# One layernorm a slot sooner, mixer pieces cut 2-3-0, the last rest products moved, and a copy moved to VectorE, in a fused attention, mixer and MLP kernel

## The chip, the cores and the metric

One NeuronCore of a Trainium2 chip runs the whole kernel. The metric is the device time of one launch in microseconds. Engines are called as in the profile: PE (TensorE matmul; PEld its weight loads), DVE (VectorE), ACT (ScalarE), POOL (GpSimd) and SP (SyncE, which here only issues DMAs).

## The reference

With 2048 rows of 576 columns in bf16:

```python
xn = layernorm(A_x)
# A: attention of 32 query heads over 16 cached key/value heads, the last 512 keys of 2048
q  = (xn @ wq).reshape(B, Sq, 32, 128)
p  = softmax(einsum(q, k) * 128 ** -0.5)
s  = (p @ v).reshape(B, Sq, 4096) @ wo
# B: mixer, then MLP
h  = gelu(layernorm(xn) @ w1)
hs = concat(the four quarters of h's columns, shifted by 1, -1, 2, -2 rows) @ w2
x1 = xn + hs
h2 = gelu(layernorm(x1) @ w3) @ w4          # 576 -> 4608 -> 576
out = A_x + s * silu(x1 + h2)
```

## The kernel before

The rows are worked in four blocks of 512. The first part of the program is attention with the mixer woven in, the second the MLP with the final product. A block and a query head make a unit; there are U = 128 of them (4 blocks x 32 heads), and the loop at L787 gives each a slot `u`, numbered from 0, with two more stretches behind the last.

In slot u PE does, in this order: the first of four scores matmuls of unit u (`stage_s`, L471: keys of 128 positions times q, each followed by an exp on ScalarE), the q projection of unit u+1 (`stage_q`, L448), the second scores, half of the value products of unit u-1 (`stage_v`, L484; 16 matmuls in all, each of which reads the exps), the third scores, the other half, and the fourth scores. What is called scores 0 to 3 in the prediction are these four. Scores have three PSUM banks, q and the mixer's pieces share two (`ps_pq`). 576 is four times 128 and 64 more: the last 64 rows of q's weights, the rest rows, are done for four heads at once (`rest_q`, L435), in every fourth slot from slot 7 on; it takes a q bank and two scores banks more, and in these slots the second scores stand right behind the first (`trip`, L693). Slot 127 has no q projection.

Other work is laid into the slots by hand. `fill` holds what is done after the first scores (layernorm steps, transposes, loads); `pe_fill` holds lists of PE matmuls, which the loop cuts into thirds and puts behind the second, third and fourth scores. Such lists are the output projection (`wo_atoms`, 32 matmuls a list, the last list 128), the mixer's first products `b1` (five matmuls to a piece, whose last starts the gelu chain `gelu1`: a cast and four more steps on VectorE around a tanh on ScalarE), and its second products `b2` (five matmuls to a tile) with `b2_rem` (20 matmuls, the last 64 columns, then one add and the store of x1). The mixer works on xnnT, the transposed result of the second layernorm: `ln2_steps` writes xnn_b on VectorE from slot `ln2_at[b]` on, three steps to a slot, and `tr2` (L555) has SP issue one DMA transpose for 128 rows, in the slots `tr2_at[b]`. Block 1's first piece stands in slot Hq + 12 = 44 (Hq is 32). At the end of each slot SP is given the DMA transpose of a finished head's output (`stage_t`, oT), which the output projection of the block reads from 32 slots later on.

SP, POOL and PE run in the order written (L786). The order on VectorE and ScalarE is a planner's, by its own costs and by priorities; exps have none, q's copies, the value results and the gelu chain have a raised one. At the start, up to L785, all engines run in the order written. There `ln1_first` (L358) normalizes the first block, and PE transposes it (`tr1_first`, L401), between transposes of the keys (`keys_first`). The tile xn has 640 columns: 576 and a second copy of the last 64 (`D:DP`), the rest columns; the copy was computed on POOL for each of the four groups of 128 rows.

Of the kernel before, what the change touches and what calls it, by code (L numbers as in the profile page):

```python
# [8 lines left out]
P = 128  # L9
ACT = mybir.ActivationFunctionType  # L10
ALU = mybir.AluOpType
# [20 lines left out]
def kernel(  # L32
# [14 lines left out]
    nc = tc.nc  # L47
# [3 lines left out]
    _, S, D = A_x.shape  # L51
    _, Hkv, Sk, Dh = A_k_cache.shape
    assert Dh == P
    Hq = A_wq.shape[1] // Dh
# [8 lines left out]
    NB = S // QB  # L63
    TB = QB // P
    SCALE = float(Dh) ** -0.5
    NF = D // P
    DR = D - NF * P
    NDC = NF + 1
    DP = NDC * P
# [26 lines left out]
    def rows(ap, t0, n):  # L96
        return ap[t0 * P:(t0 + n) * P, :].rearrange("(tt p) d -> p tt d", p=P)
# [110 lines left out]
    with ExitStack() as actx:  # L208
# [97 lines left out]
        def late(ap, fn):  # L306
            g = nc.gpsimd.tensor_copy(out=gate[:, :], in_=ap)
            with tc.issue_after(g.ins):
                fn()
# [48 lines left out]
        def ln1_first():  # L358


            x, xn = x_t.pop(0), xn_b[0]
            xn_t[0] = xn
            root = float(D) ** 0.5
            mv = small.tile([P, TB, 2], FP32, name="ln_mv")
            nb = small.tile([P, 1], FP32, name="nr_e")
            y = small.tile([P, TB], FP32, name="nr_y")
            scrap = wo_sb[:, 0:2, :].rearrange("p a b -> p (a b)").bitcast(FP32)
            t = TB - 1
            nc.scalar.activation(out=y[:, 0:1], in_=eps_t[:], func=ACT.Sqrt)
            nc.scalar.activation(out=scrap, in_=x[t], func=ACT.Copy, scale=-1.0 / (D * root), accum_out=nb[:])  # L370
            nc.scalar.activation(out=scrap, in_=x[t], func=ACT.Square, scale=1.0 / root, bias=nb[:],
                                 accum_out=mv[:, t, 1:2])
            hw = D // 2
            for i in range(t):
                st = small.tile([P, 2, 6], FP32, name="ln_st")
                for j in range(2):
                    nc.vector.bn_stats(out=st[:, j, :], in_=x[i][:, j * hw:(j + 1) * hw])
                nc.vector.bn_aggr(out=mv[:, i, :], in_=st[:])
                if i == 1:
                    nc.scalar.activation(out=y[:, 0:2], in_=mv[:, 0:2, 1], func=ACT.Sqrt, bias=eps_t[:])  # L380
            nc.vector.tensor_scalar(out=mv[:, t, 0:1], in0=nb[:], scalar1=-root, scalar2=None, op0=ALU.mult)
            nc.scalar.activation(out=y[:, 2:4], in_=mv[:, 2:4, 1], func=ACT.Sqrt, bias=eps_t[:])
            e = small.tile([P, 1], FP32, name="nr_e")
            nc.scalar.activation(out=e[:], in_=nb[:], func=ACT.Exp, scale=0.0)
            for i in range(TB):
                if i % 2 == 0:
                    nc.vector.reciprocal(out=y[:, i:i + 2], in_=y[:, i:i + 2])
                nc.gpsimd.tensor_scalar(out=xn[:, i, D:DP], in0=x[i][:, NF * P:D], scalar1=mv[:, i, 0:1],
                                        scalar2=y[:, i:i + 1], op0=ALU.subtract, op1=ALU.mult)
                nc.vector.tensor_scalar(out=xn[:, i, 0:D], in0=x[i], scalar1=mv[:, i, 0:1], scalar2=y[:, i:i + 1],  # L390
                                        op0=ALU.subtract, op1=ALU.mult)
            return mv

        def transpose_tile(dstT, src, tt):
# [156 lines left out]
        def ln2_steps(b):  # L551
            return layernorm_steps(small, [xnn_b[:, tt, 0:D] for tt in range(TB)],
                                   [xn_t[b][:, tt, 0:D] for tt in range(TB)])

        def tr2(b, tt):  # L555
            transpose_tile(xnnT, xnn_b, tt)
# [45 lines left out]
        def b2_shift(b):  # L602
            with tc.high_priority(offset=HP):
                b2_shift_(b)
# [10 lines left out]
        def b2_mm(ps, b, tt, c, lo, hi):  # L615
            if c < 4:
                o0 = PAD - SHIFT[c] + tt * P
                lhsT = hb_t[b][:, c, o0:o0 + P]
            else:
                lhsT = hs_t[b][:, tt * P:(tt + 1) * P]  # L620
            nc.tensor.matmul(ps, lhsT=lhsT, rhs=w2_sb[:, c, lo:hi], start=(c == 0), stop=(c == 4))  # L621
# [15 lines left out]
        def b2_rem(b):  # L637
            st = {}

            def mm(tt, c):  # L640
                if tt == 0 and c == 0:
                    st["ps"] = ps_pq.tile([P, TB, R0], FP32, name="psx1r", tag="pq")
                b2_mm(st["ps"][:, tt, :], b, tt, c, M0, D)
                if tt == TB - 1 and c == 4:
                    with tc.high_priority(offset=HP):
                        nc.vector.tensor_tensor(out=x1o_t[b][:, :, M0:D], in0=st["ps"][:, :, :],
                                                in1=xn_t[b][:, :, M0:D], op=ALU.add)
                    nc.sync.dma_start(out=rows(x1_dram, b * TB, TB), in_=x1o_t.pop(b)[:])
                    xn_t.pop(b)

            return [lambda tt=tt, c=c: mm(tt, c) for tt in range(TB) for c in range(5)]
# [19 lines left out]
        U = NB * Hq  # L671
        fill, pe_fill = {}, {}

        def at(u, fn):
            fill.setdefault(u, []).append(fn)

        def pe(u, atoms):
            pe_fill.setdefault(u, []).extend(atoms)
# [5 lines left out]
        def later(u, make, per):  # L684
            cell = []
            for i in range(2 * TB + 1):
                def step(i=i):
                    if not cell:
                        cell.append(make())
                    cell[0][i]()  # L690
                at(u + i // per, step)

        def trip(u):  # L693
            return PLAIN - 1 <= u < U - 1 and u % 4 == 3

        ln2_at = (7, Hq + 4, 2 * Hq - 4, 2 * Hq + 21)
        tr2_at = ((33, 33, 34, 34), (Hq + 8, Hq + 8, Hq + 9, Hq + 9),
                  (2 * Hq - 1, 2 * Hq - 1, 2 * Hq, 2 * Hq), (2 * Hq + 25, 2 * Hq + 25, 2 * Hq + 26, 2 * Hq + 26))
        b1_early = {Hq + 4: [(0, 0)], Hq + 5: [(0, 2)], Hq + 6: [(0, 4)]}
        b1_after = {Hq + 4: [(0, 1)], Hq + 5: [(0, 3)]}  # L700
# [4 lines left out]
        for c, u in enumerate((12, 13, 14, 16, 17)):  # L705
            b1_after[Hq + u] = [(1, c)]
        b2_at = ((Hq + 20, Hq + 21, Hq + 22, Hq + 24), (2 * Hq + 8, 2 * Hq + 9, 2 * Hq + 10, 2 * Hq + 12),
                 (3 * Hq + 8, 3 * Hq + 9, 3 * Hq + 10, 3 * Hq + 12), (4 * Hq - 4, 4 * Hq - 3, 4 * Hq - 2, 4 * Hq - 1))
# [12 lines left out]
        for b in range(NB):  # L721
            later(ln2_at[b], lambda b=b: ln2_steps(b), 3)
            for tt in range(TB):
                at(tr2_at[b][tt], lambda b=b, tt=tt: tr2(b, tt))
            at(b2_at[b][0] - 1, lambda b=b: b2_shift(b))
            for tt in range(TB):
                pe(b2_at[b][tt], b2(b, tt))
            pe(b2_at[b][TB - 1], b2_rem(b))
            if b + 1 < NB:
                at(x_at[b], lambda b=b: late(pT_t[x_at[b]][0][0:1, 0:1], lambda: load_x(b + 1, nc.gpsimd)))  # L730
                u1 = ln1_at[b]
                later(u1, lambda b=b: ln1_steps(b + 1), 3)
                for tt in range(TB):
                    at(u1 + (3 + tt // 2 if b else 5 + tt), lambda b=b, tt=tt: tr1(b + 1, tt))
# [24 lines left out]
        with tc.manual_schedule(engines={SP, POOL, PE, DVE, ACTE}):  # L759
            mv = ln1_first()  # L760
# [25 lines left out]
        with tc.manual_schedule(engines={SP, POOL, PE}):  # L786
            for u in range(0, max(max(fill), max(pe_fill)) + 1):  # L787
                atoms = pe_fill.get(u, []) + [fn for v, g in pe_late if v == u for fn in prep_k(g)]
                n = len(atoms)
                cut = [atoms[0:n // 3], atoms[n // 3:2 * n // 3], atoms[2 * n // 3:]]  # L790
                if u == 1:
                    stage_q(2)
                for i in range(4):
                    if u < U and not (i == 1 and trip(u)):
                        stage_s(u, i)
                    if i == 0:
                        if trip(u):
                            stage_s(u, 1)
                        if 1 < u < U - 1:
                            stage_q(u + 1)  # L800
                        for fn in fill.get(u, []):
                            fn()
                        continue
                    if i < 3 and 0 <= u - 1 < U:
                        stage_v(u - 1, 2 * (i - 1))
                    for fn in cut[i - 1]:
                        fn()
                if 0 <= u - 1 < U:
                    stage_t(u - 1)


    with ExitStack() as bctx:
# [184 lines left out]
        with tc.manual_schedule(engines={PE, DVE, ACTE}):  # L997
# [7 lines left out]
            for d in range(0, ND, 2):  # L1005
                b = d // NP
# [56 lines left out]
            b = NB - 1  # L1063
# [49 lines left out]
    with tc.If(flag > 0):  # L1113
        with ExitStack() as gctx:
# [19 lines left out]
            with tc.For_i(0, NT, 1) as t:  # L1134
# [3 lines left out]
                xn = work.tile([P, D], BF16, name="r_xn")  # L1138
# [6 lines left out]
                for h in range(Hq):  # L1145
                    g = h // REP
                    if h % REP == 0:
                        k_nat = work.tile([P, KCH, Dh], BF16, name="r_k")
                        nc.sync.dma_start(out=k_nat[:],
                                          in_=A_k_cache[0, g, K0:, :].rearrange("(kc p) d -> p kc d", p=P))  # L1150
                        v_g = work.tile([P, KCH, Dh], BF16, name="r_v")
                        nc.sync.dma_start(out=v_g[:],
                                          in_=A_v_cache[0, g, K0:, :].rearrange("(kc p) d -> p kc d", p=P))
# [80 lines left out]
```

## Time and profile before

| | before |
|---|---|
| time, median of 3 runs | 834.55 us (833.75 to 834.86) |
| the profiled execution | 833.96 us, its span 832.2 us |
| instructions | 19602 |
| granted TensorE clock | 0.998 |
| DMA | 83.95 MB, mean 101 GB/s |

The span runs from the first to the last instruction. Attention with the mixer takes the first 510 us, the last block's output projection follows up to 541, and the MLP runs from there to 825 us. In the timelines the columns are: start in us, duration in us, engine, line, operation, out<-in, shape, count; in brackets the idle time of the engine ahead of it and what ended it. SPq and POOLq stand for issues by these engines' queues. The end of a matmul is modelled, and matmuls overlap; their starts are recorded.

### The profile page before, as it was taken

How to read it: one execution, taken by the hardware profiler on the slowest of the kernel's cores; microseconds unless marked ns; L12 is line 12 of the kernel's file. 1: busy time of each engine (PE TensorE's matmuls, PEld its weight loads, DVE VectorE, ACT ScalarE, POOL GpSimd, SP SyncE). 2: the span in 40 equal slices, each digit the busy share in tenths (PEclk: the TensorE clock that was granted, in tenths of full speed). 3: DMA queues.
4: the chain of work that ended last, by engine and by line, in shares of the span. 5: the costliest groups of instructions: out<-in, count | busy, mean ns of one | idle time of the engine just before them, and what ended most of it. 6: DMA issues, size and time to landing. Idle time of an engine off the chain costs nothing.

```text
span 832.2 us, 19602 instructions
## 1 busy us (share of the span) xinstructions
PE 821.2 (99%) x7974; PEld 470.8 (57%) x7974; DVE 471.7 (57%) x1430; ACT 457.1 (55%) x819; POOL 98.7 (12%) x166
## 2 busy tenths in 40 slices
PE   9999999999999999999999999999999999999996
PEld 6666655655554565655465655555555555555555
DVE  5778635768884367964346774043246636546333
ACT  6888853578783368984467983042233333335600
POOL 5343313010100111110001100000000000000000
PEclk9999999999999999999999999999999999999999
DMA  7988992363472135772044364992000411230101
GB/s 202 188 180 187 188 170 74 85 116 71 98 148 57 41 91 124 136 139 49 12 84 128 99 112 96 313 329 34 2 28 18 98 36 45 48 87 23 37 18 44
DMA packets 141024, 83.95 MB, mean 101 GB/s; under 512 B 107504, under 2 KB 133808, under 8 KB 140928
## 3 DMA queue, kind: packets, MB, share of 16 engines
q1 hardware_dynamic: 130128, 53.01, 31.7%
q0 software_dynamic: 9408, 28.15, 12.3%
q8 instruction: 64, 1.05, 0.6%
q10 hardware_dynamic: 1392, 1.48, 0.5%
q14 instruction: 32, 0.26, 0.1%
HBM read 49.17 MB, written 9.44 MB: 70 GB/s over the span
## 4 chain that ended last, share of the span: by engine, by line
PE 97%; DVE 1%; POOL 1%; ACT 1%; issue 1%; DVEq 0%; POOLq 0%; ACTq 0%
PE ph L884 14%; PE po L494 14%; PE pswo L518 13%; PE psq L456 13%; PE sc L477 13%; PE pm L921 11%; PE pm L1086 4%; PE ph L570 3%; PE pm L884 2%; PE psx L621 2%; PE pswr L518 2%; PE pr L921 1%; PE psq L441 1%; PE sc L441 1%; PE pr L1086 0%
## 5 line engine op out<-in xcount | busy, mean ns | idle before, releaser
L479 ACT ACTIVATE pT<-sc 128x512 bf16<-128x512 f32 x512 | 287.4, 598 | 105.5 <-PE sc L477 97.4
L477 PE MATMUL sc<-qT,kT 128*128 128x512 bf16 x512 | 175.6, 379 | 0.0
L494 PEld LDWEIGHTS <-pT 128*128 128x128 bf16 x2048 | 134.5, 98 | 54.7 <-issue 9.8
L494 PE MATMUL po<-v_sb,pT 128*128 128x129 bf16 x2048 | 158.2, 220 | 0.3 <-ACT pT L479 0.3
L456 PE MATMUL psq<-xT_b,wq_b 128*128 128x512 bf16 x520 | 132.9, 379 | 0.0
L884 PE MATMUL ph<-xT_b,w_s 64*128 64x512 bf16 x976 | 127.1, 376 | 0.4 <-DVE hx L900 0.4
L921 PE MATMUL pm<-w_s,h 64*128 64x512 bf16 x864 | 122.3, 377 | 0.0
L518 PE MATMUL pswo<-wo_sb,oT 128*128 128x512 bf16 x512 | 116.6, 379 | 0.0
L499 DVE TENSOR_TENSOR o<-po,ri_b 128x256 bf16<-128x256 f32 x256 | 107.9, 422 | 6.2
L902 ACT ACTIVATE h<-ph 128x512 bf16<-128x512 f32 x67 | 39.4, 597 | 130.4 <-PE ph L884 130.4
L921 PEld LDWEIGHTS <-h 64*128 64x128 bf16 x1728 | 70.8, 94 | 55.6 <-issue 0.4
L518 PEld LDWEIGHTS <-oT 128*128 128x128 bf16 x1024 | 65.2, 98 | 56.9 <-DMA oT<-o 0.3
L921 PE MATMUL pr<-w_s,h 64*128 64x64 bf16 x864 | 90.2, 189 | 0.2 <-ACT h L902 0.2
L884 PEld LDWEIGHTS <-w_s 64*128 64x128 bf16 x1152 | 57.3, 94 | 48.9 <-issue 0.8
L456 PEld LDWEIGHTS <-wq_b 128*128 128x128 bf16 x520 | 50.5, 98 | 59.5 <-issue 1.0
L900 DVE COPY hx<-ph 128x512 f32<-128x512 f32 x55 | 38.0, 691 | 70.0 <-PE ph L884 70.0
L498 DVE RECIPROCAL ri_b<-po 128x2 f32<-128x2 f32 x256 | 42.2, 165 | 52.9 <-PE po L494 48.9
L477 PEld LDWEIGHTS <-kT 128*128 128x128 bf16 x512 | 47.0, 98 | 24.5 <-DVE qT L464 0.6
L265 POOL DMA_DIRECT2D wq_b<-in_A_wq_dram x30 | 23.3, 777 | 293.4 <-PE sc L477 273.9
L464 DVE TENSOR_TENSOR qT<-psq,rq 128x512 bf16<-128x512 f32 x60 | 41.4, 690 | 23.6 <-ACT pT L479 13.2
L466 DVE CAST qT<-psq 128x512 bf16<-128x512 f32 x44 | 30.3, 688 | 34.4 <-PE psq L441 27.3
L874 DVE TENSOR_SCALAR fence<-ph,ph 1x1 f32<-1x1 f32 x61 | 12.8, 209 | 51.7 <-PE ph L884 51.1
(151 smaller groups left out, 755.3 us busy)
## 6 DMA issues: line engine op xcount, KB each, us to landing
wq_b<-in_A_wq_dram POOLq DMA_DIRECT2D x30, 512.0 KB, 4.8
wo_sb<-in_A_wo_dram POOLq DMA_DIRECT2D x8, 576.0 KB, 5.3
w_s<-in_B_w_dram SPq DMA_DIRECT2D x9, 512.0 KB, 7.1
w_s<-in_B_w_dram SPq DMA_DIRECT2D x10, 288.0 KB, 5.1
x_dram<-x SPq DMA_DIRECT2D x4, 576.0 KB, 3.4
x<-x_dram SPq DMA_DIRECT2D x4, 576.0 KB, 4.2
w_s<-in_B_w_dram SPq DMA_DIRECT2D x4, 576.0 KB, 7.7
s_b<-s_dram SPq DMA_DIRECT2D x4, 576.0 KB, 5.0
```

Source lines behind the costliest of these rows:

```text
L456: nc.tensor.matmul(psq[:, :], lhsT=w[:, kc, hh * Dh:(hh + 1) * Dh], rhs=xT_b[qb % 2][:, kc, :], start=(kc == 0 and not (two and hh == 1)), ...
L464: nc.vector.tensor_tensor(out=qT[:, :], in0=psq[:, :], in1=rq_t.pop(u)[:, :], op=ALU.add)
L477: nc.tensor.matmul(sc[:, :], lhsT=kT[:, g, kc * P:(kc + 1) * P], rhs=qT_t[u][:, :], start=True, stop=True)
L479: nc.scalar.activation(out=pT[:, :], in_=sc[:, :], func=ACT.Exp, scale=SCALE)
L494: nc.tensor.matmul(po[:, j, :], lhsT=pTs[kc][:, tt * P:(tt + 1) * P], rhs=v_sb[:, g, kc, 0:Dh + 1], start=(kc == 0), stop=(kc == KCH - 1))
L498: nc.vector.reciprocal(out=ri, in_=po[:, :, Dh])
L499: nc.vector.tensor_tensor(out=o[:, t0:t0 + 2, :], in0=po[:, :, 0:Dh], in1=ri.unsqueeze(2).to_broadcast([P, 2, Dh]), op=ALU.mult)
L518: nc.tensor.matmul(ps, lhsT=oT_t[qb * Hq + h][:, tt, :], rhs=wo_sb[:, h, lo:hi], start=(h == 0), stop=(h == Hq - 1))
L884: nc.tensor.matmul(ps[i][:, :], lhsT=lhsT, rhs=xT[half, kc, :], start=first, stop=last, skip_group_check=True)
L900: nc.vector.tensor_copy(out=src[:, :], in_=ps[i][:, :])
L902: nc.scalar.activation(out=h3[:, :], in_=src[:, :], func=ACT.Gelu_apprx_tanh)
L921: nc.tensor.matmul(out, lhsT=h3_t[b, fc][half, tt * P:(tt + 1) * P], rhs=w4_s[fc // WS][half, fc % WS, lo:hi], start=key not in started, s ...
```

## The change

- `ln2_at[1]` is 35 instead of 36 (the second layernorm of block 1), and `tr2_at[1]`, its four DMA transposes, 39, 39, 40, 40 instead of 40, 40, 41, 41.
- A list of exactly five matmuls is cut 2, 3, 0 instead of 1, 2, 2. This meets the mixer's pieces and tiles that stand alone in a slot.
- `b2_rem` of the last block leaves the thirds of slot 127 and stands in `fill` of slot 128, where it comes ahead of the value products of unit 127. Slot 127 then has a list of five.
- For row groups 2 and 3 of the first block POOL no longer computes the rest columns; VectorE copies them for both groups at once from columns 512 to 575 of the finished xn.

```diff
                 if i % 2 == 0:
                     nc.vector.reciprocal(out=y[:, i:i + 2], in_=y[:, i:i + 2])
-                nc.gpsimd.tensor_scalar(out=xn[:, i, D:DP], in0=x[i][:, NF * P:D], scalar1=mv[:, i, 0:1],
-                                        scalar2=y[:, i:i + 1], op0=ALU.subtract, op1=ALU.mult)
+                if i < 2:
+                    nc.gpsimd.tensor_scalar(out=xn[:, i, D:DP], in0=x[i][:, NF * P:D], scalar1=mv[:, i, 0:1],
+                                            scalar2=y[:, i:i + 1], op0=ALU.subtract, op1=ALU.mult)
                 nc.vector.tensor_scalar(out=xn[:, i, 0:D], in0=x[i], scalar1=mv[:, i, 0:1], scalar2=y[:, i:i + 1],
                                         op0=ALU.subtract, op1=ALU.mult)
+            nc.vector.tensor_copy(out=xn[:, 2:TB, D:DP], in_=xn[:, 2:TB, NF * P:D])
...
-        ln2_at = (7, Hq + 4, 2 * Hq - 4, 2 * Hq + 21)
-        tr2_at = ((33, 33, 34, 34), (Hq + 8, Hq + 8, Hq + 9, Hq + 9),
+        ln2_at = (7, Hq + 3, 2 * Hq - 4, 2 * Hq + 21)
+        tr2_at = ((33, 33, 34, 34), (Hq + 7, Hq + 7, Hq + 8, Hq + 8),
...
-            pe(b2_at[b][TB - 1], b2_rem(b))
+            if b + 1 < NB:
+                pe(b2_at[b][TB - 1], b2_rem(b))
+            else:
+                for atom in b2_rem(b):
+                    at(U, atom)
...
-                cut = [atoms[0:n // 3], atoms[n // 3:2 * n // 3], atoms[2 * n // 3:]]
+                c1, c2 = (2, n) if n == 5 else (n // 3, 2 * n // 3)
+                cut = [atoms[0:c1], atoms[c1:c2], atoms[c2:]]
```

## The prediction

> **What bounds the kernel now.** I read the page first, then the waits of PE, then the timeline at each place that the change touches.
>
> ```profile
> span 832.2 us, 19602 instructions
> PE 821.2 (99%) x7974; PEld 470.8 (57%) x7974; DVE 471.7 (57%) x1430; ACT 457.1 (55%) x819; POOL 98.7 (12%) x166
> ...
> L494 PE MATMUL po<-v_sb,pT 128*128 128x129 bf16 x2048 | 158.2, 220 | 0.3 <-ACT pT L479 0.3
> ```
>
> PE is never idle for long: 99% of the span. Nothing taken off DVE, ACT or POOL shortens the run by itself; only a place where PE stands still does. The change removes no matmul and adds none, so its whole worth is the sum of the PE pauses that it closes, less those that it opens. PE's waits name one large one in the attention phase:
>
> ```profile
> PE ph L570 <- issue: 1.4, 1, 1.4
> ```
>
> It is the first matmul of block 1's first mixer piece (slot 44). The timeline around it (start, duration, engine, line):
>
> ```profile
> 148.59 1.45 DVE L136 TENSOR_SCALAR xnn_b<-xn_b,ln_mv,nr_y 128x576 bf16<-128x576 bf16 x4
> ...
> 161.08 3.11 SPq L507 DMA_TRANSPOSE oT<-o  x2
> 164.24 2.59 SPq L395 DMA_TRANSPOSE xnnT<-xnn_b  x2
> 166.94 1.20 SPq L507 DMA_TRANSPOSE oT<-o  x1
> 168.18 2.60 SPq L395 DMA_TRANSPOSE xnnT<-xnn_b  x2
> ...
> 169.12 0.79 POOL L265 DMA_DIRECT2D wq_b<-in_A_wq_dram  x1 [13.98 <-PE sc L477]
> ...
> 170.67 1.02 PE L456 MATMUL psq<-xT_b,wq_b 128*128 128x512 bf16 x4
> ...
> 172.16 0.63 PE L494 MATMUL po<-v_sb,pT 128*128 128x129 bf16 x8
> ...
> 174.81 0.62 PE L494 MATMUL po<-v_sb,pT 128*128 128x129 bf16 x8
> ...
> 176.81 0.38 PE L570 MATMUL ph<-xnnT,w_sb 128*128 128x512 bf16 x1 [1.38 <-issue]
> ```
>
> The matmul reads xnnT, written by four DMA transposes. Two answers on that tile say how long these took to land, first the third transpose, then the third and fourth together:
>
> ```profile
> L395 SPq DMA_TRANSPOSE xnnT<-xnn_b x1: 1275/1275/1275, 168.2 to 168.2; - x1
> DMA to landing us min/median/max: 2.6/2.6/2.6
> ...
> L395 SPq DMA_TRANSPOSE xnnT<-xnn_b x2: 1275/1276/1276, 168.2 to 169.5; - x2
> DMA to landing us min/median/max: 2.6/4.9/7.2
> ```
>
> The fourth, issued at 169.5, needs 7.2 us and lands at 176.7; PE goes on at 176.81. The third, one issue earlier, needed 2.6. Between them the load of wq begins (169.12). The layernorm is not late: its results were written by 150.0, 14 us before the first transpose. What is late is the transposes' place in SP's queue.
>
> **Part 1: second layernorm and transposes of block 1.** The eight value products from 174.81 show 0.62 us, one alone 0.22 (the page's row of L494): starts 0.057 apart, the last at 175.21, so PE could have gone on at 175.27. Lost: 176.81 - 175.27 = 1.54 us. SP's order after the projection's store is now oT, oT, two xnnT, oT, two xnnT; afterwards oT, two xnnT, oT, two xnnT, oT. The fourth xnnT moves ahead of one oT, whose issue holds SP for 1.2 to 1.3 us, so it is issued at about 168.2. That is the time at which the third went out before, and it then landed in 2.6: 170.8, or 4.5 us before PE asks. The wq load does not move, since it waits for PE (its row). I take the full 1.54. The oT transposes that are passed go out later and meet the load in its place; block 1's output projection reads them only from slot 65 on. The layernorm's VectorE work is the same and has 14 us of slack. If the cover fails (issue after 169.1), the whole 1.54 stays. The edit frees nothing else: next late are the two pauses of part 2.
>
> A page speaks to the size. The Trainium skill (Trainium Kernel Development and Optimization, Performance Expectations) calls matmul busy time a bad metric because matmuls are pipelined. By the idle time of the row, 1.38, the sum below would be 0.16 smaller; the starts, which the trace has for every matmul, decide for 1.54.
>
> **Part 2: five-matmul pieces in two thirds of a slot.** A slot runs: scores 0, q, scores 1, half of the value products, third one, scores 2, other half, third two, scores 3, third three. Five matmuls were cut 1, 2, 2 and become 2, 3, 0. This concerns 18 slots (44 to 46, 48, 49, 52 to 54, 72 to 74, 104 to 106, 124 to 127). From 170.67 the four q matmuls show 1.02 us, the last one 0.38, so starts are 0.215 apart. The piece's last matmul comes one step, 0.215, sooner; scores 3 comes two steps, 0.43, later; the slot is as long as before.
>
> For it: two pauses where every fourth slot takes the rest rows of q. An undisturbed one runs from its q matmuls to its value products in 172.16 - 170.67 = 1.49 us. Those of slots 47 and 51:
>
> ```profile
> 186.62 1.03 PE L456 MATMUL psq<-xT_b,wq_b 128*128 128x512 bf16 x4
> 187.26 0.69 DVE L585 CAST g_x<-ph 128x512 bf16<-128x512 f32 x1
> 188.52 0.63 PE L494 MATMUL po<-v_sb,pT 128*128 128x129 bf16 x8
> ...
> 200.41 1.02 PE L456 MATMUL psq<-xT_b,wq_b 128*128 128x512 bf16 x4
> 200.51 0.63 ACT L591 ACTIVATE g_th<-g_u 128x512 bf16<-128x512 bf16 x1 [0.36 <-DVE g_u L589]
> 201.04 1.55 ACT L479 ACTIVATE pT<-sc 128x512 bf16<-128x512 f32 x3
> 202.47 0.63 PE L494 MATMUL po<-v_sb,pT 128*128 128x129 bf16 x8
> ```
>
> Slot 47 takes 1.90 (0.41 lost): q's second bank is the piece's, free when the cast ends at 187.95. Slot 51 takes 2.06 (0.57 lost): the tanh at 200.51 holds up three exps, and their banks are wanted. Both hang on the gelu chain, which starts with the piece's last matmul. Bounds: nothing (the chain is held by VectorE's order, or scores 3 comes too late in slot 46) to 0.98. A chain that is 0.215 sooner all through gives back 0.22 at each place, 0.43; the steps that a planner orders may give more or less. I take 0.45.
>
> Against it: the 0.43 by which scores 3 is late. Its exp starts 0.42 after the matmul and serves PE 0.65 after that (507.88, 508.30, 508.95 in the rows below): 1.07 in all. In an ordinary slot the value products that need it follow seven steps and three small ones later, 7 x 0.215 + 3 x 0.057 = 1.7: covered by ScalarE being at most 0.6 behind. In slot 46 it is busy 2.69 of 3.71 us:
>
> ```profile
> 182.48:186.19 3.71, 3.71 (x30) 2.18 (x29) 3.50 (x11) 2.69 (x5) 1.98 (x3) 1.00 0.32 75
> ```
>
> (after the window: its length, then PE, PEld, DVE, ACT). So I cost it at nothing there. Slot 127 has no q, and the cover is gone.
>
> **Parts 2 and 3 at the end of attention.** The rows of slots 127 and 128:
>
> ```profile
> 504.64 1.73 ACT L479 ACTIVATE pT<-sc 128x512 bf16<-128x512 f32 x3 [0.44 <-PE sc L477]
> 504.87 0.59 PE L477 MATMUL sc<-qT,kT 128*128 128x512 bf16 x2
> 505.31 0.62 PE L494 MATMUL po<-v_sb,pT 128*128 128x129 bf16 x8
> ...
> 507.88 0.38 PE L477 MATMUL sc<-qT,kT 128*128 128x512 bf16 x1
> 508.22 0.28 PE L621 MATMUL psx1r<-w_sb,hb 128*128 128x64 bf16 x4
> 508.30 0.60 ACT L479 ACTIVATE pT<-sc 128x512 bf16<-128x512 f32 x1 [0.24 <-PE sc L477]
> 508.36 0.33 PE L494 MATMUL po<-v_sb,pT 128*128 128x129 bf16 x3
> 508.95 0.91 PE L494 MATMUL po<-v_sb,pT 128*128 128x129 bf16 x13 [0.26 <-ACT pT L479]
> 509.02 0.36 SPq L648 DMA_DIRECT2D x_dram<-x  x1
> 509.50 3.00 SPq L507 DMA_TRANSPOSE oT<-o  x2
> ```
>
> Now: the third small value product starts at 508.47, the fourth could at 508.53 and waits until 508.95: 0.42 lost. The 20 rest products (64 columns, 0.03 apart by 508.22: 0.58 in all) stood 3, 8 and 9 in the thirds of slot 127; afterwards all stand behind scores 3. Behind it come one step, 0.58 and three small products, 0.97, against 1.07: 0.10 lost. So part 3 gains 0.32. But scores 3 of slot 126 is late by 0.43: its exp starts at 505.07 instead of 504.64, serves PE at 505.72, and the fourth value product from 505.31 wants it at 505.48. That opens 0.24. Net of the two at this place: 0.08. I take 0.1.
>
> On SP the store of x1 (509.02) falls from before the last two oT transposes to between them; it waits for one VectorE add behind the rest products. Behind it on SP stands only the last oT.
>
> **Part 4: rest columns on VectorE.** The start (PE's transposes of x, then q):
>
> ```profile
> 9.28 1.09 DVE L412 COPY xT_b<-ps_x 128x512 bf16<-128x512 bf16 x3 [0.90 <-PE ps_x L404]
> 9.36 0.10 PEld L404 LDWEIGHTS <-xn_b 128*128 128x128 bf16 x1 [0.18 <-POOL xn_b L388]
> 9.39 1.08 ACT L410 ACTIVATE xT_b<-ps_x 128x512 bf16<-128x512 bf16 x2 [0.93 <-PE ps_x L404]
> 9.88 2.32 PE L456 MATMUL psq<-xT_b,wq_b 128*128 128x512 bf16 x10
> ```
>
> One transpose waits 0.18 for POOL; that wait goes. But q's fourth matmul needs ScalarE's second copy, done at 10.47, and starts at 9.88 + 3 x 0.215 = 10.53. It cannot come 0.18 sooner, only about 0.03. VectorE's added copy (between nothing and the 0.42 of one of its copies here) lies in the 0.90 us in which VectorE waits. POOL's next work, a load of v, starts sooner by the two instructions that leave it; its heads come up many slots later. Bounds 0 to 0.18; I take 0.03, by the copy's row.
>
> **Sum.** 1.54 + 0.45 + 0.1 + 0.03 = 2.1 us. The profiled execution took 833.96 us (span 832.2, the rest outside it), the median of the three runs is 834.55. So a span of about 830.1, 831.9 for such an execution, and 832.4 on the median.
>
> **Rivals.**
> - *The pieces give nothing* (pauses at 47 and 51 stay, 0.1 at the end stays or goes): 1.5 to 1.7 us, 832.9. For it: the chain has planner-ordered steps between cast and tanh. Against: its first link is plainly PE. A part of it: the last oT was issued as the second of the 3.00 us at 509.50, and PE wants it 31 steps after 509.7, at 516.4; if it lands no sooner while PE comes sooner, the gain of part 3 returns as a wait.
> - *The transpose still meets the load*: issue slips past 169.1, it lands at 176.7, 1.54 is lost and 0.6 remains: 833.9. Against: SP's issues are back to back and one of them is taken from in front. The Trainium skill (DMA: Bandwidth & Descriptors, Queues, rings and completion order) says that each DMA engine takes turns between queues packet by packet, so any transpose unfinished when the load starts would be stretched; the 7.2 beside 2.6 agrees, and by that rule only an issue ahead of the load helps.
> - *Slower: late scores 3 everywhere.* If ScalarE is over 0.6 us behind at scores 3, each of the other 17 slots opens the 0.24 of slot 127: 4.1 us, net 2.0 slower, 836.5. For it: tanh and q copies share ScalarE in five of them. Against: 2.69 of 3.71 busy, and plain slots run scores 3 right before the next slot without a pause.
>
> **How the numbers follow.** Forecast 0.57, pieces give nothing 0.28, load still met 0.09, slower 0.06. The bound of 0.2% is 1.7 us, about what a measurement of this kernel can tell from no change. The forecast lies beyond it except for a twentieth (0.54), the first rival on either side of it (0.13 faster, 0.15 same), the second within. Faster 0.67, same 0.27, slower 0.06. Range: the pieces' full 0.98 and some scatter below, 831.4; the met load above, 833.9.
>
> **What would show it.** Right: no wait of ph L570 on issue; the fourth xnnT of block 1 issued near 168.2 and landed in under 3 us; slots 47 and 51 nearer 1.49 from q to value products; a new pause of about 0.24 in slot 127's first value products; q at the start moved by under 0.1. Wrong: a landing over 5 us for that transpose, or new pauses of PE before value products in slots 45 to 50, which would be the slower case.

## The result, and the profile after

| | before | after |
|---|---|---|
| median | 833.70 us (9 runs, 832.97 to 834.86) | 831.54 us (9 runs, 831.07 to 831.96) |
| profiled execution | 833.96 us, span 832.2 | 831.61 us, span 829.8 |
| ratio of the times | | 0.9972, 95% interval 0.9962 to 0.9983 |

By the medians the change saves 2.16 us; the ratio puts it at 0.28%. (The first three runs of before had 834.55, the median that the prediction was set against.) The top of the page after, and PE's waits after:

```profile
span 829.8 us, 19512 instructions
...
PE 816.6 (98%) x7888; PEld 471.4 (57%) x7974; DVE 472.8 (57%) x1431; ACT 455.3 (55%) x819; POOL 97.2 (12%) x164
```

```profile
PE ph L891 <- DVE hx L907: 0.4, 2, 0.2
PE pr L928 <- ACT h L909: 0.2, 1, 0.2
```

PE's busy time says nothing here: this trace lacks 86 matmul records (7888 against 7974). The weight loads (PEld) are complete, and all shifts below are taken from their starts, before against after. The wait of ph on issue is gone from the list, and with it the wait of po on pT at the end of attention; the shorter waits that came in its place are told below. Two waits of ph on hx are left, at 575 and 709 us; they play a part below.

**Block 1's transposes.** The third and fourth after:

```profile
L397 SPq DMA_TRANSPOSE xnnT<-xnn_b x2: 1275/1280/1285, 167.0 to 168.3; - x2
...
DMA to landing us min/median/max: 2.6/2.6/2.7
```

The fourth is issued at 168.3 and lands after 2.7 us where it took 7.2. From slot 44 to slot 45 the weight loads shift by 1.54.

**Slots 46, 47 and 51** (timeline after):

```profile
184.04 0.63 ACT L593 ACTIVATE g_th<-g_u 128x512 bf16<-128x512 bf16 x1 [0.82 <-DVE g_u L591]
...
184.57 2.04 ACT L481 ACTIVATE pT<-sc 128x512 bf16<-128x512 f32 x4
184.63 0.95 PE L479 MATMUL sc<-qT,kT 128*128 128x512 bf16 x3
...
185.42 1.02 PE L458 MATMUL psq<-xT_b,wq_b 128*128 128x512 bf16 x4
185.76 0.69 DVE L587 CAST g_x<-ph 128x512 bf16<-128x512 f32 x1
...
187.03 0.63 PE L496 MATMUL po<-v_sb,pT 128*128 128x129 bf16 x8
...
198.70 0.74 PEld L458 LDWEIGHTS <-wq_b 128*128 128x128 bf16 x4
198.74 0.63 ACT L593 ACTIVATE g_th<-g_u 128x512 bf16<-128x512 bf16 x1
...
200.70 0.63 PE L496 MATMUL po<-v_sb,pT 128*128 128x129 bf16 x8
```

Slot 47 now needs 187.03 - 185.42 = 1.61 us from q to its value products (1.90 before, 1.49 undisturbed). But on ScalarE the tanh of 184.04 now stands ahead of the exps of the third and fourth scores of slot 46: ScalarE waits 0.82 for the tanh's input, and four exps follow in a row from 184.57 on. (Before, the exp of the third scores ran at 184.92, ahead of the tanh at 185.66.) So the second scores of slot 47 find no free bank in time: they start at 185.21, when the exp of the third scores is done (185.15), 0.37 behind the first instead of the 0.22 of before, and q comes 0.15 late with them. Net gain at this place: 0.15. In slot 51 q's first weight load stands at 198.70, which puts its first matmul at 198.91 (0.21 later, as in slot 47: 185.21 and 185.42), so 1.79 us against 2.06: 0.27 gained.

**The end of attention** (timeline after):

```profile
503.34 1.57 ACT L481 ACTIVATE pT<-sc 128x512 bf16<-128x512 f32 x3 [0.66 <-PE sc L479]
...
503.57 0.88 PE L496 MATMUL po<-v_sb,pT 128*128 128x129 bf16 x8
503.99 0.28 PEld L496 LDWEIGHTS <-pT 128*128 128x128 bf16 x5 [0.26 <-ACT pT L481]
...
506.45 0.60 ACT L481 ACTIVATE pT<-sc 128x512 bf16<-128x512 f32 x1 [0.66 <-PE sc L479]
```

Eight value products take 0.88 instead of 0.62: the new pause of slot 127, 0.25, with its releaser named. In slot 128 the fourth value product, which needs the last exp, still waits 0.10 and starts at 507.10. Together the place gains 0.11 to 0.13.

**The start.** First before, then after:

```profile
9.25 1.75 POOL L288 DMA_DIRECT2D v_sb<-in_A_v_cache_dram  x2
```

```profile
8.11 1.75 POOL L288 DMA_DIRECT2D v_sb<-in_A_v_cache_dram  x2
...
8.51 0.57 DVE L393 COPY xn_b<-xn_b 128x128 bf16<-128x128 bf16 x1
...
8.79 0.86 PE L406 MATMUL ps_x<-ident,xn_b 128*128 128x128 bf16 x10
```

The moved copy takes 0.57 us, and PE's transposes wait for it for 0.12. The first q matmul starts at 10.00 instead of 9.88, but 0.10 of this is the first loads: PE's first transpose of x stands at 7.26 instead of 7.16. Counted from that transpose, the first q matmul comes 0.01 to 0.02 later, and q's third weight load and all behind it 0.13 later (3.07 against 2.94).

All shifts together, up to the last matmul (825.16 before, 823.33 after): 1.54 + 0.42 + 0.11 - 0.13, less the 0.10 by which the first loads landed later, is 1.84; the last matmul shows 1.83. The rest of the 2.35 us between the spans lies behind the start of the last matmul (7.03 us before, 6.50 after), where the profiles of all kernels here lie anywhere between 6.0 and 7.0.

### The profile page after: what moved, and what is told of

Its sections match the earlier page's. It is cut to its first block, busy times and chain, and to the rows that moved or that the text cites. A ratio compares the mean times of both kernels' runs of the same rounds, so it can differ in the third digit from the quotient of the medians.

```text
span 829.8 us, 19512 instructions
## 1 busy us (share of the span) xinstructions
PE 816.6 (98%) x7888; PEld 471.4 (57%) x7974; DVE 472.8 (57%) x1431; ACT 455.3 (55%) x819; POOL 97.2 (12%) x164
## 4 chain that ended last, share of the span: by engine, by line
PE 96%; DMA 1%; issue 1%; DVE 1%; ACT 1%; POOL 0%; ACTq 0%; POOLq 0%; DVEq 0%
PE ph L891 14%; PE po L496 14%; PE pswo L520 13%; PE sc L479 13%; PE psq L458 13%; PE pm L928 11%; PE pm L1093 4%; PE ph L572 3%; PE pm L891 2%; PE psx L623 2%; PE pswr L520 2%; PE pr L928 1%; PE psq L443 1%; PE sc L443 1%; DMA wo_sb<-in_A_wo_dram 1%
## 5 line engine op out<-in xcount | busy, mean ns | idle before, releaser
L479 PE MATMUL sc<-qT,kT 128*128 128x512 bf16 x509 | 171.8, 379 | 0.1
L458 PE MATMUL psq<-xT_b,wq_b 128*128 128x512 bf16 x469 | 126.1, 379 | 2.7
L520 PE MATMUL pswo<-wo_sb,oT 128*128 128x512 bf16 x500 | 114.9, 379 | 0.6
```

The lines of the kernel that those rows point to most:

```text
L458: nc.tensor.matmul(psq[:, :], lhsT=w[:, kc, hh * Dh:(hh + 1) * Dh], rhs=xT_b[qb % 2][:, kc, :], start=(kc == 0 and not (two and hh == 1)), ...
L479: nc.tensor.matmul(sc[:, :], lhsT=kT[:, g, kc * P:(kc + 1) * P], rhs=qT_t[u][:, :], start=True, stop=True)
L520: nc.tensor.matmul(ps, lhsT=oT_t[qb * Hq + h][:, tt, :], rhs=wo_sb[:, h, lo:hi], start=(h == 0), stop=(h == Hq - 1))
```

## Experiments

Each kernel is `before` with the edit that is shown, unless it says otherwise; the times stand beside runs of `before` on the same chip.

**One part at a time.**

Part 1, the layernorm and the transposes:

```diff
-        ln2_at = (7, Hq + 4, 2 * Hq - 4, 2 * Hq + 21)
-        tr2_at = ((33, 33, 34, 34), (Hq + 8, Hq + 8, Hq + 9, Hq + 9),
+        ln2_at = (7, Hq + 3, 2 * Hq - 4, 2 * Hq + 21)
+        tr2_at = ((33, 33, 34, 34), (Hq + 7, Hq + 7, Hq + 8, Hq + 8),
```

> Part 1 alone (the layernorm and the transposes of block 1 a slot sooner). Theory of pauses: the 1.54 us pause at block 1's first mixer piece goes and nothing else moves; the fourth transpose is issued near 168.2 and lands in 2.6 us, PE's starts behind it come 1.54 sooner, time about 1.5 us below before. Rival (the load of wq is met by whatever is then in flight, and the next consumer waits in its place): a new pause of a like size appears within 20 us, time within 0.5 us of before.

831.49 against 833.75: ratio 0.9972, interval 0.9961 to 0.9983. The step at slot 45 is 1.54. Alone it measures as much as the whole change, which its 1.54 does not explain. Its trace has two more steps of 0.35 each in the MLP, at 577 and 711 us of before: there the waits of ph on hx are gone.

Part 2, the cut:

```diff
-                cut = [atoms[0:n // 3], atoms[n // 3:2 * n // 3], atoms[2 * n // 3:]]
+                c1, c2 = (2, n) if n == 5 else (n // 3, 2 * n // 3)
+                cut = [atoms[0:c1], atoms[c1:c2], atoms[c2:]]
```

> Part 2 alone (five-matmul lists cut 2, 3, 0). Theory of pauses: slots 47 and 51 lose about 0.4 us less between them, but a new pause of about 0.25 us opens in slot 127, where scores 3 of slot 126 comes 0.43 late; net 0.2 to 0.25 us below before. Rival (the late scores 3 costs everywhere): pauses of 0.1 to 0.3 us before value products in most of the 17 other slots, time 1 us or more above before.

833.15 against 833.75: 0.9995, 0.9986 to 1.0004. Slot 47 gains 0.15, slot 51 0.27, the end of attention loses 0.20. (Slot 44, whose wait for the transpose is still there, takes 0.19 more than in before; the wait shows 1.6 instead of 1.4.) No pause opens before the value products of the other slots.

Part 3, the rest products:

```diff
-            pe(b2_at[b][TB - 1], b2_rem(b))
+            if b + 1 < NB:
+                pe(b2_at[b][TB - 1], b2_rem(b))
+            else:
+                for atom in b2_rem(b):
+                    at(U, atom)
```

> Part 3 alone (last block's rest products behind the last scores, lists still cut 1, 2, 2). Theory of pauses: with two matmuls of the list and the 20 rest products behind the last scores there are 1.4 us of work against the 1.07 us that an exp needs, so the whole 0.42 us pause in slot 128 goes, and there is none in slot 127: 0.42 below before, more than the 0.13 that the end of attention gained in the changed kernel. Rival (the store of x1 between the last two oT transposes delays the last one): a pause of 0.3 us or more in the last output projection, time equal to before.

833.32 against 833.75: 0.9993, 0.9984 to 1.0002. In the trace the end of attention gains 0.43, and the wait of po on pT is gone from PE's list: without the new cut nothing of the 0.42 is left over.

Part 4, the copy:

```diff
-                nc.gpsimd.tensor_scalar(out=xn[:, i, D:DP], in0=x[i][:, NF * P:D], scalar1=mv[:, i, 0:1],
...
+                if i < 2:
+                    nc.gpsimd.tensor_scalar(out=xn[:, i, D:DP], in0=x[i][:, NF * P:D], scalar1=mv[:, i, 0:1],
...
+            nc.vector.tensor_copy(out=xn[:, 2:TB, D:DP], in_=xn[:, 2:TB, NF * P:D])
```

> Part 4 alone (rest columns of two row groups by a VectorE copy). Theory (the copy is slow, 0.57 us in the changed kernel, and PE's transposes wait for it): PE's first q matmul and what follows come 0.1 to 0.15 us later counted from the first transpose of x; time 0.1 above before, under what the rounds resolve. Rival (the later start in the changed kernel was the scatter of the first loads): counted from the first transpose of x, the q matmuls start no later than before.

832.70 against 833.75: 0.9990, 0.9982 to 0.9999. Its own place loses 0.13 to 0.15, which the wait in slot 44 takes up again (1.1 instead of 1.4). Yet the kernel is faster than that explains: the two MLP waits are gone here too. So parts 1 and 4 each come with 0.70 that stands in neither edit, and the whole change, which holds both, does not have it.

**Was the layernorm late, or only the transposes' place?**

```diff
-        tr2_at = ((33, 33, 34, 34), (Hq + 8, Hq + 8, Hq + 9, Hq + 9),
+        tr2_at = ((33, 33, 34, 34), (Hq + 7, Hq + 7, Hq + 8, Hq + 8),
```

> Only the slots of the four xnn transposes of block 1 move (slots 39, 39, 40, 40 instead of 40, 40, 41, 41); the layernorm stays in slot 36, the pieces, the last mixer products and the copy as before. Theory: the layernorm was not late, only the fourth transpose stood behind the wq load in SP's queue; then the fourth transpose is issued before that load, lands within 3 us of its issue instead of 7.2, the wait of the first mixer product in slot 44 goes, and the weight loads of slot 45 start 1.54 earlier, as in the run with both moved. Rival: the layernorm's rows were what the transpose waited for; then its issue stays at 169.5 or later, it lands at 176 to 177 and nothing is gained (833.7 by the median of before). The two pauses of 0.35 in the MLP at the hx copy can come or go with this build by the count of VectorE's instructions ahead of it: theory 832.2 with them, 831.5 without.

832.16 against 833.81 (0.9981, 0.9972 to 0.9991), with the MLP waits. The third and fourth transposes:

```profile
L395 SPq DMA_TRANSPOSE xnnT<-xnn_b x2: 1276/1276/1277, 167.0 to 168.3; - x2
...
DMA to landing us min/median/max: 2.6/2.6/2.7
```

The same step of 1.54; 0.60 of it is lost again where PE reads the last oT. So the layernorm's slot is worth nothing at this place. What it did in part 1 alone was to take one instruction out of VectorE's stream (1786 there, 1787 here), and that counts in the MLP, as shown below.

**Is it the wq load that stretches the fourth transpose?** The transposes stay, the load is held back:

```diff
-            at(4 * (j - 1) - 1, lambda j=j: load_wq(j))
+            if j == 12:
+                at(45, lambda j=j: late(pT_t[45][0][0:1, 0:1], lambda: load_wq(j)))
+            else:
+                at(4 * (j - 1) - 1, lambda j=j: load_wq(j))
```

> Layernorm and transposes of block 1 stay where they were; the wq load that meets the fourth transpose is held until the first exp of slot 45, some 10 us later. Theory (the two transfers share the queues' time and the transpose is slow because of the load): the transpose is issued at about 169.5 as before, lands in under 3.5 us instead of 7.2, and slot 44's pause goes: 1.3 to 1.55 less at slot 45, 832.2 to 832.4 by the median of before (0.7 less without the two MLP pauses). Rival (the transpose is slow by its own place or by its issue): it still lands at 176 to 177 and the time is 833.7. Danger in this edit, not in the theory: the load itself may then come late for its projection.

832.82 against 833.81 (0.9990, 0.9981 to 1.0).

```profile
L395 SPq DMA_TRANSPOSE xnnT<-xnn_b x2: 1275/1276/1276, 168.2 to 169.5; - x2
...
DMA to landing us min/median/max: 2.6/3.5/4.3
```

Issued at 169.5 as before, the fourth now lands in 4.3 us instead of 7.2, in time for PE, and the step at slot 45 is the full 1.54. So the collision with that load made the pause. It was expected to land in under 3.5; what stretches it by the 1.7 over the usual 2.6 is not settled. The time was expected at 832.2 to 832.4: of the gain 0.34 was lost again in slot 47 and 0.26 at the last oT.

**Why does the copy take 0.57 us?** Part 4, and the v load that GpSimd issues beside the copy held back until slot 1:

```diff
-                at(2 * g - 8, lambda g=g: load_v(g // 2))
+                if g == 4:
+                    at(1, lambda g=g: late(pT_t[1][0][0:1, 0:1], lambda: load_v(g // 2)))
+                else:
+                    at(2 * g - 8, lambda g=g: load_v(g // 2))
```

> The copy of x's rest columns on VectorE as in the change (alone), and the v load that GpSimd issued at 8.11 while the copy ran is held until the first exp of unit 1. Theory (the copy was slow because it shared the SBUF port with GpSimd's work): the copy takes 0.15 to 0.3 instead of 0.57, the fifth transpose no longer waits and PE's first q products start 0.1 to 0.17 sooner than in the run of part 4 alone, compared from the end of the first transposes. Rival (0.57 is the copy's own time on 2 x 64 columns): it stays within 0.5 to 0.6 and PE's wait of 0.12 to 0.17 stays. Time of the whole: within 0.3 of the run of part 4 alone (832.7) if the MLP pauses are absent as there, 833.4 with them.

832.68, as the run of part 4 (832.70), in which slot 44's wait still takes up what is lost or won ahead of it. Timeline of part 4 alone, then of this kernel:

```profile
8.02 1.75 POOL L288 DMA_DIRECT2D v_sb<-in_A_v_cache_dram  x2
...
8.42 0.57 DVE L393 COPY xn_b<-xn_b 128x128 bf16<-128x128 bf16 x1
...
8.71 0.85 PE L406 MATMUL ps_x<-ident,xn_b 128*128 128x128 bf16 x10
```

```profile
8.35 0.20 DVE L393 COPY xn_b<-xn_b 128x128 bf16<-128x128 bf16 x1
...
8.63 0.72 PE L406 MATMUL ps_x<-ident,xn_b 128*128 128x128 bf16 x10
```

By itself the copy takes 0.20, and the ten transposes 0.72 instead of 0.85. Counted from PE's first transpose of x, q's third weight load stands at 2.93, as in before (2.94): without the issue beside it the moved copy costs nothing, and gains nothing. In the slow case it ends with the issue of the first of GpSimd's two DMAs (8.02 + 0.98 = 9.00 and 8.42 + 0.57 = 8.99; in the changed kernel 9.09 and 9.08). The Trainium skill (SBUF — State Buffer, SBUF: two separate sides) says that VectorE in some modes and GpSimd hold a shared port pair as an exclusive lock for a whole instruction, the later one blocked until the first is done. The runs agree that the one holds up the other: 0.57 beside the issue, 0.20 without it. But by that rule the copy would be done about 0.2 behind the issue (an estimate from the copy's own time), and it ends with it; so what in the issue holds it is not shown.

**The two MLP waits: an instruction that does nothing.** In VectorE's recorded stream the two late copies to hx are instructions 1344 and 1600 in every kernel with the waits (before, after, parts 2 and 3, the transposes alone, the held load). In part 1 alone the stream is one instruction shorter, in part 4 alone one longer, and there the waits are missing. So, on `before`:

```diff
     nc.vector.memset(eps_t[:], LN_EPS)
+    one_t = const.tile([P, 1], FP32, name="one_t")
+    nc.vector.memset(one_t[:], 1.0)
```

> The kernel before with one more VectorE instruction at its very start, a memset of a 128x1 tile that nobody reads; nothing else is changed. Theory (the two MLP pauses come from where an instruction falls in VectorE's stream: the late hx copies are number 1344 and 1600 of its recorded instructions, 256 apart, and in the builds without the pauses other instructions have these numbers): the copies become number 1345 and 1601, start 0.04 after their wait's end instead of 0.40, both PE pauses of 0.35 go, and the time falls by 0.70, to 833.0 against 833.7, for an instruction that does nothing. Rival (the pauses are made by what the builds with them have in common in time, such as a transfer that meets the copy): they stay and the time is 833.7.

832.91 against 833.81 (0.9991, 0.9982 to 1.0). Timeline of before, then of this kernel:

```profile
576.13 0.60 ACT L902 ACTIVATE h<-ph 128x512 bf16<-128x512 f32 x1 [2.54 <-PE ph L884]
...
576.52 0.69 DVE L900 COPY hx<-ph 128x512 f32<-128x512 f32 x1 [2.04 <-PE ph L884]
...
577.26 0.61 PE L884 MATMUL ph<-xT_b,w_s 64*128 64x512 bf16 x4 [0.20 <-DVE hx L900]
```

```profile
576.05 0.60 ACT L904 ACTIVATE h<-ph 128x512 bf16<-128x512 f32 x1 [2.54 <-PE ph L886]
...
576.08 0.69 DVE L902 COPY hx<-ph 128x512 f32<-128x512 f32 x1 [1.68 <-PE ph L886]
...
576.83 0.39 PE L886 MATMUL ph<-xT_b,w_s 64*128 64x512 bf16 x2
```

Before, the copy starts 0.39 behind the activation that is released with it; now 0.03. The copies are numbers 1345 and 1601, both steps of 0.35 are there, and PE's two waits are gone. So the position makes the pause.

The same instruction, here in the changed kernel:

```diff
     nc.vector.memset(eps_t[:], LN_EPS)
+    one_t = const.tile([P, 1], FP32, name="one_t")
+    nc.vector.memset(one_t[:], 1.0)
```

> The changed kernel with the same one VectorE memset at its start. Theory (position in VectorE's stream): the hx copies that were number 1344 and 1600 become 1345 and 1601, both MLP pauses of 0.35 go and the time falls by 0.70 against the changed kernel beside it: 830.8 if that one is at 831.5. Rival (the pauses went in the earlier run for another reason): they stay, 831.5.

831.20 against 833.74 (0.9962, 0.9948 to 0.9976), 0.59 below the changed kernel beside it; both steps of 0.35 are in the trace. Its profiled execution, the longest of five with 833.05, shows what else can happen: a transpose of block 1's xn landed late in a crowded stretch at 100 us.

```profile
PE psq L460 <- DMA xT_b<-xn_b: 1.9, 1, 1.9
```

The changed kernel once more, on that chip:

> The changed kernel once more, as it is, so that it stands beside the others on the same chip: 831.5, with both MLP pauses of 0.35, the copy of x's rest columns at 0.57 and the pauses of 0.25 and 0.10 at the end of attention.

831.79 against 833.74 (0.9974, 0.9964 to 0.9984), with the pauses of its first profile. The shift to the last matmul is 2.03 us; of the 0.20 between the two profiles 0.18 lies at the start, in the landing of the first loads.

**A better version.** Parts 1 and 3 as shown above, no copy, and the cut only where it paid:

```diff
-                cut = [atoms[0:n // 3], atoms[n // 3:2 * n // 3], atoms[2 * n // 3:]]
+                c1, c2 = (2, n) if u in (44, 45, 48) else (n // 3, 2 * n // 3)
+                cut = [atoms[0:c1], atoms[c1:c2], atoms[c2:]]
```

> Parts 1 and 3 of the change, the pieces in two thirds only in slots 44, 45 and 48, and no part 4. Against the changed kernel: the pause of 0.25 in slot 127 should not come (0.13 better at the end of attention: the third part alone took 0.39 there, the change 0.13, so 0.26 at most), slot 47's new wait of 0.15 should not come, and the start saves the copy's 0.12: 0.4 to 0.5 less. If its hx copies are not number 1344 and 1600 in VectorE's stream, another 0.70 less. So 831.1 with the MLP pauses, 830.4 without, where the changed kernel is at 831.5. Rival (the pieces must be finished early in slots 46 and 49 too, or the pause at the end comes from part 3 alone): 831.5 with the pauses, 830.8 without.

830.02 against 833.74: 0.9952, 0.9938 to 0.9965; 1.77 below the changed kernel beside it. Its stream holds 1786 VectorE instructions, the hx copies are numbers 1343 and 1599, and the MLP waits are gone. The second scores of slot 47 do not wait (that place gains 0.26 instead of 0.15), which confirms that the cut in slot 46 made them late, and slot 127 has no pause:

```profile
503.44 0.62 PE L494 MATMUL po<-v_sb,pT 128*128 128x129 bf16 x8
```

The end of attention gains 0.43, as part 3 alone did, so the pause of 0.25 and the 0.10 left over both came from the cut in slots 126 and 127. What its trace also shows is the last oT transpose: issued 508.40, landed 514.53, and PE waits.

```profile
PE pswo L518 <- DMA oT<-o: 0.3, 1, 0.3
```

This takes 0.47 in the profiled execution, the longest of the five (830.84). Between this trace and that of the changed kernel on the same chip the last matmul differs by only 0.47 (822.65 and 823.12); without the 0.47 of oT and the 0.26 by which its first transpose of x starts later it would be 1.20, and the terms give about as much, 1.25: 0.69 of the MLP waits, 0.32 at the end of attention, 0.11 in slot 47, 0.13 of the copy. The rest of the 1.77, some 0.5, is not placed.

## Why the prediction was right or wrong

Part 1 came as forecast. Three steps failed: the base of the time (834.55 from three runs, where nine had 833.70), the bound on the moved copy in part 4 (forecast 0.03 gained, measured 0.13 lost), and in part 2 the late scores of slot 46, costed at nothing (measured 0.15).

- **Part 1, 1.54:** right to the hundredth, and by its mechanism: 168.3 for the issue, 2.7 us to land, and the held load shows the collision. By starts was the right way to size it; the idle time of 1.38 in the row was too small. That queues take turns packet by packet, as the Trainium skill (DMA: Bandwidth & Descriptors, Queues, rings and completion order) has it, agrees with 4.3 us without the load and 7.2 beside it; no run here shows the alternation itself.
- **Part 2, 0.45:** the sum was right (0.42) by luck, the split was not. Slot 51 gave 0.27 for 0.22. Slot 47's pause shrank by 0.29, but the step "I cost it at nothing there" (the late fourth scores of slot 46) failed: 0.15 came back as a wait of the next scores. The argument was ScalarE's busy share of that slot, 2.69 of 3.71 us, in the order of before. With the new cut the order itself is another: the tanh stands ahead of the exps of the third and fourth scores, and ScalarE waits for it idle. The pauses gave 0.56 for the 0.43 reckoned, the scores took 0.15 for nothing, and the two errors cancel.
- **End of attention, 0.1:** 0.11 to 0.13, with the pause of 0.24 (0.25) and the 0.10 left where they were forecast.
- **Part 4, +0.03:** wrong in sign; it costs 0.13. The step that failed is the bound on the copy, "between nothing and the 0.42 of one of its copies", and beside it the sentence on POOL. That sentence saw that the v load would start sooner and asked only when its data are used. It starts at 8.11 instead of 9.25, beside the copy, and the copy takes 0.57. Nor do the runs show the 0.03: with the copy at 0.20, q comes no sooner than before.
- **The sum, 2.1:** measured 2.16 by the medians, 1.83 in the trace up to the last matmul. The terms as measured add up to 1.94 (1.54 + 0.42 + 0.11 - 0.13). That the medians agree with the forecast better than its terms do is at least partly scatter: 0.52 of the trace's 2.35 lies behind the last matmul.
- **The time, 832.4:** 0.86 above what came, nearly all of it the base: 834.55 was the median of three runs, nine had 833.70, and 2.1 less is 831.6. The spread of those three (1.1 us) was half of the gain that was forecast. The profiled execution of before, at 833.96, was already nearer. The measured gain lies between 0.17% and 0.38%, so whether it is beyond the prediction's bound of 0.2%, to which it gave a chance of 0.67, is not settled.
- **The rivals:** the pieces did not give nothing, the transpose did not meet the load, and the late scores of no slot but 46 and 126 opened a pause. The oT landing named in the first rival is real: against before, PE loses 0.16 to 0.60 where it reads the last oT in six of the profiles (parts 1 and 4, the transposes alone, the held load, the memset on before, the better version), though not in those of the changed kernel.
- **Not in the prediction:** the two MLP waits. They stood in PE's waits of before and, being outside the change, were not priced. Their 0.70 is more than parts 2 to 4 gave together (0.40). The change left them where they were only because its parts shift VectorE's count by +1 and -1: luck, as far as the prediction goes.

## What to carry to other kernels

Price a moved issue twice: by what it now lands ahead of, and by what the engine that it left does next and beside whom; the first gave 1.54 us, the second turned the moved copy from worth nothing into a loss of 0.13. Test one part at a time, and count the instructions of each engine's stream: here one more or one fewer moved the time by 0.70 us, so a part tried alone seemed worth half again its true gain. Take the base from enough runs that its spread is small beside the effect.

## What the runs showed of the hardware

- **A border in VectorE's stream.** Where recorded instruction 64 of a group of 128 stands directly behind its own wait, it starts 0.396 us after the wait's end; the other hx copies directly behind a wait do so after 0.042 to 0.044, but for the first of them in each profile (0.79). In the thirteen profiles a distance of 0.395 to 0.397 behind a wait shows at instructions 448, 960, 1088, 1344 and 1600, and at no other; number 192, behind a wait in five of them, does not show it. In before a packet of 8192 bytes in an instruction queue starts 0.67 to 0.69 us after the start of numbers 448, 1344 and 1600. The Trainium skill (Perfetto Trace Analysis, The 4-stage abstract model) gives an instruction 64 bytes; by that one packet would be 128 instructions (an estimate), which agrees with the 256 between the two late copies. When the instruction at the border is a wait, nothing is lost: with the memset on before, number 1344 is the copy's own wait; in part 1 alone it is the wait behind the copy, which is recorded 0.39 us after the copy's start instead of 0.04, while the copy runs. That the fetching of the next packet makes the pause fits all of this; no run shows it directly.
- **A DMA issue on GpSimd can hold up VectorE.** A copy of 128 columns took 0.57 us beside it and 0.20 without.
- **A transpose that meets a load of wq** took 7.2 us to land, 4.3 with that load held back, and 2.7 when issued 1.2 us sooner.
